# DeltaNet and a multiplicative FFN on one core: another list of steps, with ScalarE's copies of w3 slabs ahead of the first inverse

## The chip, the core and the metric

The kernel runs on one NeuronCore of one Trainium2 chip. The core has five engines that work through their own instruction queues side by side: TensorE (PE in the profile, with its weight loads as PEld), VectorE (DVE), ScalarE (ACT), GpSimd (POOL) and SyncE (SP, which here only issues DMAs). An engine takes its instructions strictly in the order in which the program lists them, and an instruction that needs something from another engine waits at the head of its queue, with everything behind it. The metric is the device time of one execution in microseconds (us).

## What is computed

The reference has two blocks, one behind the other, all in float32. The inputs are q, k, v of shape (4, 8, 768, 48) (batch, heads, tokens, features), beta of (4, 8, 768), and the weights w1, w2 (384 x 1024), w3 (1024 x 1024) and w_out (1024 x 384).

```python
k_n = k / (norm(k) + 1e-6)
for t in range(768):                       # for each batch and head, state is 48 x 48
    y[t]  = q[t] @ state
    state = state + beta[t] * outer(k_n[t], v[t] - k_n[t] @ state)
x = y as (3072 tokens, 384)                # heads side by side
out = ((x @ w1) * (x @ w2)) @ w3 @ w_out   # (3072, 384)
```

## The kernel before

**The recurrence** is done in 12 chunks of 64 tokens. For a chunk, a matrix of products of keys is built for every batch and head, its unit triangular inverse is found, and a few small matmuls then give the chunk's outputs and the next state. Inverses are found for two chunks at a time, on VectorE: a step of elimination is two VectorE instructions (L484 and L489 for the first two pairs of chunks), 31 steps for a pair. The matrix under elimination lies in PSUM, in one of the two double banks that the other small matmuls of the recurrence share.

**The FFN** is linear in h = (x @ w1) * (x @ w2), so w3 @ w_out is multiplied out once: "the fold". w3 comes in 16 pieces of 128 x 512. TensorE transposes each piece (L842), ScalarE brings the result out of PSUM into SBUF (L845), and for each of eight slabs of 128 rows TensorE then accumulates eight matmuls of 384 columns (L856), one for each slab of w_out. The tokens are then worked off 512 at a time (u = 0 to 5): products with w1 and w2, and products with the folded weights. From u = 1 on, and for the folded weights, both use a scheme of Strassen's kind with fewer products and more additions.

All weights arrive as 64-bit pieces of another coding and are turned into float32 on the way: ScalarE does two instructions on a piece (L799, L800), VectorE two (L802, L803), GpSimd one (L807).

**The order of the work** is written out by hand: `ORDER` is a list of 1458 names. Each name stands for a small generator, and each time a name comes up, that generator runs on to its next `yield`; it so adds some instructions to one engine's queue, or to two. At the end `in_text_order()` makes each engine keep exactly this order. In this document P7.3 is the third time that P7 comes up. The names that the change and the prediction speak of are:

- `P0` to `P7`, pieces of w_out; `P8` to `P23`, pieces of w3 (two for each slab of rows: P8 and P9 are slab 0); `P24` to `P35`, pieces of w1 and w2. Each has four steps: .1 the DMA (SP), .2 two ScalarE instructions, .3 two VectorE instructions, .4 one GpSimd instruction. The raw data lie in five buffers that are taken in turn, so the DMA of a piece waits for step .4 of the fifth piece before it.
- `t0` to `t15`: .1 the four transposes of one piece of w3, .2 ScalarE's copy of them into SBUF (L845). t4 and t5 belong to slab 2, t2 and t3 to slab 1.
- `f0` to `f7`: the fold of a slab, .1 its first four and .2 its last four matmuls (two records each in the profile), .3 ScalarE's copy of the result (L863).
- `s m`, `u m`: products of keys of chunk m, with their scaling on VectorE (L395), and the copies that put them in order for the inverse (L446, ScalarE and GpSimd).
- `V j`: the inverse of pair j. For j = 0 and 1: .1 GpSimd writes a unit matrix, .2 VectorE transposes the input (L466), .3 and .4 ScalarE copies the unit matrix into PSUM in two halves (L475), .5 to .35 are the steps of elimination, and .36 is VectorE's transpose of the result (L503).
- `e m`: the inverse is put in place and its corner completed (for chunks 0 to 3 by copies .1 on ScalarE, .2 on GpSimd, .3 on ScalarE, then .4 a VectorE transpose, L559, and from .5 on two products on TensorE with ScalarE copies behind them); `c m`: the chunk's state update, three products (L647) with VectorE work behind each (L678, L687, L707); `y m`: its outputs (L746), brought out by eight ScalarE copies (L767); `d m`: VectorE transposes of keys and queries (L339); `g j`, `N j`: squares and norms of keys; `n m`: GpSimd scales v (L633).
- `b`, `a0`: products of the tokens of u = 0 with w1 and w2 (L876), and for u of 1 to 5 `a`, `h`, `i`, `j` (L995); `S`, `o`, `x`: sums and products with the folded weights (L1105) and results.

PSUM gives the transposes, the fold and the FFN four single banks in turn: each new user waits until the one four before it has been read out.

The fold's lines, with the slab order that the first fold takes:

```python
first = not folded
turn = (0, 3, 2, 5, 1, 4, 6, 7) if first else (0, 3, 2, 1, 5, 4, 6, 7)
for i, kc in enumerate(turn):
    pe.matmul(ps[:, 0:DM], lhsT=w3Ts[jc, kc // 4][:, kc % 4 * P : kc % 4 * P + P],
              rhs=wo[:, kc], start=(i == 0), stop=(i == KF - 1))
    if i == KF // 2 - 1:
        yield
```

So the first slab that is folded needs both of its transposed pieces, and w_out's pieces 0, 3, 2 and 5, for its first half; every later one needs its first piece and w_out's 0, 3, 2 and 1.

Of the kernel before, what the change touches and what calls it, by code (L numbers as in the profile page):

```python
# [43 lines left out]
t4 V0 V0 P5 V0 V0 P4 t10 P7 P4 t3 t3 V0 V0 P1 f1 P6 P6 t4 V0 P7 V0 V0 t10 t1 P14 P7 P4 V0 f0 V0  # L44
P6 P16 P16 V0 V0 P7 t1 s0 P19 P19 P19 P19 V0 f1 P17 k3 p2 v1 V0 V0 P14 P14 P14 V0 f2 P17 f2 f0 V0
f2 P15 v0 P20 f1 t11 f0 P17 P17 f5 V0 V0 P16 t11 P16 t8 P15 V1 V0 t8 f5 t9 V0 V0 t6 P15 V0 n0 n0
f5 V0 V0 V0 V0 t9 P20 P20 V0 t6 P22 P22 P22 f4 P23 P23 V0 f4 f4 P21 P21 P15 t7 t7 V0 s1 V0 V0 V0
V0 g1 d2 d2 P22 f3 f3 P24 P20 g1 g1 p3 g1 P26 p3 P30 e0 e0 e0 t12 t14 e1 e1 g1 f3 e0 e0 d3 d3 N1
s2 s2 s2 P23 P23 t12 e0 f6 e0 p4 s2 P24 e1 e1 t14 s2 e0 P24 s2 P25 c0 P26 f7 u2 P30 P24 c0 e1 e1
P21 P21 d3 d3 y0 y0 P26 P26 P31 t15 t13 s3 s3 s3 s3 s3 s3 t13 c0 n1 n1 P32 t15 u2 u2 u3 c0 P30 f7  # L50
e1 P25 P25 P31 P31 P27 c1 c1 u3 u3 f6 e1 c1 V1 V1 V1 y0 P31 f6 f7 P25 P27 V1 V1 V1 V1 P30 b1 c1
N1 b1 v2 P32 V1 V1 P27 V1 s1 y1 y1 b2 V1 d4 V1 V1 P28 P29 P32 b2 P27 V2 V1 V1 V1 y1 b3 V1 V1 P28
P28 b0 P32 c1 b2 b2 b3 b1 b1 b0 P29 P29 b0 P29 a03 a03 a02 V1 b0 V1 d4 V1 V1 a01 V1 P28 V1 V1 a02
V1 P35 a01 a00 a00 n2 n2 a04 a04 b7 P33 P33 a05 a05 P34 P34 a01 a07 b7 V1 b4 b5 V1 V1 V1 V1 k4
a01 a07 k5 b5 b3 g2 b4 V1 V1 P35 V1 V1 g2 c1 e2 e2 e2 e2 a06 a06 g2 e3 e3 e3 b3 g2 g2 a00 a02 a02
# [12 lines left out]
V3 V3 V3 V3 oB1 xB1 xC1 S1 j20 k9 V3 xD1 V3 V3 V3 V3 S1 oC1 a20 a20 p8 xC1 V3 xC1 h20 V3 xD1 xC1
# [1226 lines left out]
```

## Time and profile before

| | us |
|---|---|
| median of 3 runs (554.44 to 555.08) | 554.49 |
| the profiled execution itself | 556.72 |
| its span, from the first to the last instruction | 555.0 |
| TensorE busy in the span | 523.2 (94%) |
| VectorE busy | 390.5 (70%) |
| GpSimd busy | 257.8 (46%) |
| ScalarE busy | 188.1 (34%) |

The span is what the views of the trace measure; 1.7 us of the profiled execution lie outside it, and it was 2.2 us longer than the median of the runs. A line of a timeline gives an instruction's start and length in us, engine, line, operation, what it writes and reads, its shape, and in square brackets the idle time of the engine before it with what ended it. A line of a table of windows gives, for one stretch, its length, each engine's busy time with the number of instructions, the granted TensorE clock (1.00 is full), the share of the DMA engines and GB/s.

### The profile page before, as it was taken

How to read it: one execution, taken by the hardware profiler on the slowest of the kernel's cores; microseconds unless marked ns; L12 is line 12 of the kernel's file. 1: busy time of each engine (PE TensorE's matmuls, PEld its weight loads, DVE VectorE, ACT ScalarE, POOL GpSimd, SP SyncE). 2: the span in 40 equal slices, each digit the busy share in tenths (PEclk: the TensorE clock that was granted, in tenths of full speed). 3: DMA queues.
4: the chain of work that ended last, by engine and by line, in shares of the span. 5: the costliest groups of instructions: out<-in, count | busy, mean ns of one | idle time of the engine just before them, and what ended most of it. 6: DMA issues, size and time to landing. Idle time of an engine off the chain costs nothing.

```text
span 555.0 us, 19886 instructions
## 1 busy us (share of the span) xinstructions
PE 523.2 (94%) x8540; PEld 449.2 (81%) x8540; DVE 390.5 (70%) x850; ACT 188.1 (34%) x393; POOL 257.8 (46%) x278
## 2 busy tenths in 40 slices
PE   2587999999999999999999999999999999999997
PEld 2473666688778988889987889988899888998897
DVE  3989999899976878659976579858587644124332
ACT  4788288954542112332021530123231121300000
POOL 8585553723658970455443255510382212341141
PEclk9987999999999999999999999999999999999999
DMA  8977976579356445345553564353421220020001
GB/s 248 240 184 195 219 161 127 124 167 146 60 81 116 87 110 81 60 97 92 99 110 61 79 113 65 108 78 47 96 51 44 59 55 4 8 67 1 0 1 57
DMA packets 197688, 52.64 MB, mean 95 GB/s; under 512 B 185345, under 2 KB 191489, under 8 KB 197601
## 3 DMA queue, kind: packets, MB, share of 16 engines
q1 hardware_dynamic: 193408, 50.59, 44.1%
q8 instruction: 67, 1.10, 0.8%
q10 hardware_dynamic: 4192, 0.79, 0.8%
q14 instruction: 21, 0.16, 0.1%
HBM read 41.25 MB, written 8.91 MB: 90 GB/s over the span
## 4 chain that ended last, share of the span: by engine, by line
PE 68%; DVE 11%; DMA 8%; ACT 7%; SPq 2%; issue 2%; POOL 1%; DVEq 0%; POOLq 0%; ACTq 0%
PE ps_f L995 32%; PE ps_f L1105 16%; PE ps_w L647 5%; DMA raw<-in_moe_w_dram 5%; PE ps_w L746 4%; PE ps_w L576 2%; PE ps_w L383 2%; PE ps_f L876 2%; PE ps_w L389 2%; PE ps_f L856 2%; DVE tb L484 1%; DVE tb L495 1%; ACT xT L767 1%; DVE ps_w L489 1%; DVE ps_w L500 1%
## 5 line engine op out<-in xcount | busy, mean ns | idle before, releaser
L1003 DVE TENSOR_TENSOR ab<-ab,ps_f 128x512 f32<-128x512 f32 x80 | 54.6, 683 | 58.1 <-PE ps_f L995 57.5
L1076 POOL TENSOR_TENSOR ab<-ab 128x512 f32<-128x512 f32 (+1 forms) x56 | 61.3, 1118 | 41.0 <-PE ps_f L1105 29.5
L995 PE MATMUL ps_f<-xT,w1s 128*128 128x256 f32 x320 | 78.5, 382 | 0.0
L1042 POOL TENSOR_TENSOR ab<-ab,late 128x512 f32<-128x512 f32 x19 | 24.1, 1270 | 108.2 <-DVE ab L1003 108.2
L995 PEld LDWEIGHTS ps_f<-xT,w1s 128*128 128x128 f32 x320 | 59.9, 190 | 7.9
L1105 PE MATMUL ps_f<-w,ab 128*128 128x192 f32 x376 | 65.6, 329 | 0.0
L1105 PEld LDWEIGHTS ps_f<-w,ab 128*128 128x128 f32 x376 | 61.3, 190 | 1.3 <-issue 0.7
L856 PE MATMUL ps_f<-w2s,w3T 128*128 128x384 f32 x128 | 46.3, 514 | 3.4 <-ACT w3T L845 3.4
L409 POOL TENSOR_TENSOR PT<-PT,smask 128x512 f32<-128x512 f32 x20 | 25.7, 1285 | 51.3 <-ACT PT L407 51.3
L1105 PE MATMUL ps_f<-room,ab 128*128 128x192 f32 x272 | 47.3, 328 | 0.0
L500 DVE TENSOR_TENSOR ps_w<-ps_w,tb 128x31 f32<-128x31 f32 (+15 forms) x124 | 43.3, 349 | 4.3
L767 ACT COPY xT<-ps_w 48x256 f32<-48x256 f32 x96 | 30.4, 365 | 45.2 <-PE ps_w L746 44.7
L495 DVE TENSOR_TENSOR tb<-ps_w,Ub 128x31 f32<-128x31 f32 (+15 forms) x124 | 42.0, 338 | 4.1 <-DMA Ub<-Ud 0.5
L1105 PEld LDWEIGHTS ps_f<-room,ab 128*128 128x128 f32 x272 | 44.3, 190 | 0.6 <-issue 0.3
L1011 ACT COPY ab<-ps_f 128x512 f32<-128x512 f32 x20 | 11.7, 586 | 94.9 <-PE ps_f L995 94.8
L995 PE MATMUL ps_f<-xT,room 128*128 128x256 f32 x160 | 41.2, 385 | 0.0
L856 PEld LDWEIGHTS ps_f<-w2s,w3T 128*128 128x128 f32 x128 | 24.7, 200 | 20.0 <-issue 5.8
L995 PE MATMUL ps_f<-xT,w2s 128*128 128x256 f32 x160 | 40.1, 381 | 0.0
L995 PE MATMUL ps_f<-x_room,w2s 128*128 128x256 f32 x160 | 38.9, 386 | 0.0
L995 PEld LDWEIGHTS ps_f<-x_room,w2s 128*128 128x128 f32 x160 | 29.5, 190 | 5.1 <-DVE late L1003 1.0
L807 POOL TENSOR_TENSOR w<-w,raw 128x512 uint32<-128x512 uint32 x16 | 21.2, 1327 | 26.8 <-DMA raw<-in_moe_w_dram 7.6
L995 PEld LDWEIGHTS ps_f<-xT,room 128*128 128x128 f32 x160 | 29.6, 190 | 4.7 <-DVE osb L1135 0.6
(146 smaller groups left out, 1024.2 us busy)
## 6 DMA issues: line engine op xcount, KB each, us to landing
raw<-in_moe_w_dram SPq DMA_DIRECT2D x16, 512.0 KB, 5.6
vtok<-in_v_dram SPq DMA_DIRECT2D x24, 192.0 KB, 4.2
raw<-in_moe_w_dram SPq DMA_DIRECT2D x24, 192.0 KB, 3.9
out_dram<-osb SPq DMA_DIRECT2D x46, 96.0 KB, 1.7
ktok<-in_k_dram SPq DMA_DIRECT2D x44, 96.0 KB, 3.1
raw<-in_moe_w_out_dram SPq DMA_DIRECT2D x8, 384.0 KB, 3.2
perm<-in_k_dram SPq DMA_DIRECT2D x40, 64.0 KB, 3.0
perm<-in_q_dram SPq DMA_DIRECT2D x32, 64.0 KB, 2.5
```

The lines of the kernel that those rows point to most:

```text
L409: pool.tensor_tensor(out=PT, in0=PT, in1=smask[:].unsqueeze(1).to_broadcast([P, H, C]), op=ALU.mult)
L495: dve.tensor_tensor(out=tv, in0=V[:, 0 : s + 1, s : s + 1].to_broadcast([P, s + 1, n]), in1=U[:, s, s + 1 : BS].unsqueeze(1).to_broadcast( ...
L500: dve.tensor_tensor(out=o, in0=o, in1=tv, op=ALU.subtract)
L647: pe.matmul(out(ps, r, h, z), lhsT=lhs(r, h, z), rhs=rhs(r, h, z), start=True, stop=True,)
L746: i = pe.matmul(region(h, z, r), lhsT=lhs, rhs=rhs, start=part[n] not in part[:n], stop=part[n] not in part[n + 1 :],)
L767: act.copy(out=xT[f, p:NP:2, b : b + NR, cc, :].rearrange("p a r t -> p r a t"), in_=pyv[f, z, b : b + NR],)
L856: pe.matmul(ps[:, 0:DM], lhsT=w3Ts[jc, kc // 4][:, kc % 4 * P : kc % 4 * P + P], rhs=wo[:, kc], start=(i == 0), stop=(i == KF - 1),)
L995: pe.matmul(acc[name][:, n * i : n * i + n], lhsT=ws[b][:, P * i : P * i + P], rhs=xs[x], start=new and k == 0 and i == 0, stop=k == len(t ...
L1003: dve.tensor_tensor(out=o_, in0=x, in1=acc[name], op=ALU.add)
L1042: eng.tensor_tensor(out=Z1, in0=Z1, in1=late, op=ALU.mult)
L1076: pool.tensor_tensor(out=o_, in0=x_, in1=y_, op=op)
L1105: pe.matmul(ps[b][:, b, :], lhsT=block(u, HF * f + i, z)[:, P * b : P * b + P], rhs=ws_[w][:, i], start=first and i == 0 and (b == 0 or n ...
```

## The change

The list is replaced from its 122nd entry on. The same 1458 names come up, each as often as before, so that the same instructions are issued; what differs is their order on each engine, and with it which PSUM bank, buffer or slab each one gets. All other code stays.

At the first difference, ScalarE's copies t3.2, t4.2 and t10.2 come directly behind u1.3. They stood behind V0.3, V0.4, P4.2 and, for the latter two, behind P6.2 and P7.2. ScalarE then goes on with V0.3, P4.2, V0.4, P6.2, P7.2, P14.2. The first fold is that of slab 2 (f2, then f0, f1, f5) where it was slab 1 (f1, then f0, f2, f5). On VectorE, P4.3 comes ahead of the first step of elimination, P14.3 and P16.3 come earlier, and P15.3 later; n0 comes behind P15.4 on GpSimd, where it stood ahead of it. The rest of the list is in another order in most of its lines. Shown are the first 15 lines and the last two that are replaced, and what takes their place (the line ahead of them, the same in both, ends with `P1 u1 u1`; the entry `t4` that the first replaced line begins with is the same too).

```diff
-t4 V0 V0 P5 V0 V0 P4 t10 P7 P4 t3 t3 V0 V0 P1 f1 P6 P6 t4 V0 P7 V0 V0 t10 t1 P14 P7 P4 V0 f0 V0
-P6 P16 P16 V0 V0 P7 t1 s0 P19 P19 P19 P19 V0 f1 P17 k3 p2 v1 V0 V0 P14 P14 P14 V0 f2 P17 f2 f0 V0
-f2 P15 v0 P20 f1 t11 f0 P17 P17 f5 V0 V0 P16 t11 P16 t8 P15 V1 V0 t8 f5 t9 V0 V0 t6 P15 V0 n0 n0
-f5 V0 V0 V0 V0 t9 P20 P20 V0 t6 P22 P22 P22 f4 P23 P23 V0 f4 f4 P21 P21 P15 t7 t7 V0 s1 V0 V0 V0
-V0 g1 d2 d2 P22 f3 f3 P24 P20 g1 g1 p3 g1 P26 p3 P30 e0 e0 e0 t12 t14 e1 e1 g1 f3 e0 e0 d3 d3 N1
-s2 s2 s2 P23 P23 t12 e0 f6 e0 p4 s2 P24 e1 e1 t14 s2 e0 P24 s2 P25 c0 P26 f7 u2 P30 P24 c0 e1 e1
-P21 P21 d3 d3 y0 y0 P26 P26 P31 t15 t13 s3 s3 s3 s3 s3 s3 t13 c0 n1 n1 P32 t15 u2 u2 u3 c0 P30 f7
-e1 P25 P25 P31 P31 P27 c1 c1 u3 u3 f6 e1 c1 V1 V1 V1 y0 P31 f6 f7 P25 P27 V1 V1 V1 V1 P30 b1 c1
-N1 b1 v2 P32 V1 V1 P27 V1 s1 y1 y1 b2 V1 d4 V1 V1 P28 P29 P32 b2 P27 V2 V1 V1 V1 y1 b3 V1 V1 P28
-P28 b0 P32 c1 b2 b2 b3 b1 b1 b0 P29 P29 b0 P29 a03 a03 a02 V1 b0 V1 d4 V1 V1 a01 V1 P28 V1 V1 a02
-V1 P35 a01 a00 a00 n2 n2 a04 a04 b7 P33 P33 a05 a05 P34 P34 a01 a07 b7 V1 b4 b5 V1 V1 V1 V1 k4
-a01 a07 k5 b5 b3 g2 b4 V1 V1 P35 V1 V1 g2 c1 e2 e2 e2 e2 a06 a06 g2 e3 e3 e3 b3 g2 g2 a00 a02 a02
-p4 v3 d4 d4 p5 a00 e2 P34 c2 c2 e2 P34 e2 b6 P35 P35 e2 c2 c2 e3 a03 g2 g2 P33 b6 y2 g2 P33 g2 d5
-d5 p5 c2 c2 y2 a04 e3 s4 N2 e3 s4 a03 s4 b6 b6 s4 s4 s4 s4 T e3 T T d5 n3 d5 a04 e3 b4 b4 b7 s5
-n3 k6 g3 u4 s5 s5 s5 s5 s5 s5 b5 b7 b5 a05 T c3 c3 a06 a05 a06 u5 V2 p6 g3 a07 a07 c3 c3 g3 S0 S0
...
-a53 a53 h53 j53 h51 h53 h53 h53 i53 i53 i53 xC4 o5 x5 o5 S5 S5 o5 o5 x5 S5 S5 S5 S5 o5 x5 x5 o5
-x5 x5 x5 x5 x5 x5 S5 o5 x5 x5 x5 x5
+t4 t10 t3 t3 t4 t10 V0 V0 P5 t1 P4 P4 P1 f2 V0 V0 P4 P7 P14 V0 P6 P6 P6 V0 V0 f0 P7 P14 P14 P16
+s1 P16 V0 P7 V0 V0 P7 P19 f2 P16 P16 f2 P17 P17 k3 P19 t1 f1 f1 V0 V0 f5 V0 f0 P19 f1 p2 v1 V0 f0
+V0 V0 V0 V0 V1 P19 t11 t11 P14 t6 P15 V0 V0 P15 s0 P17 P17 V0 V0 V0 V0 t8 t8 V0 g1 P15 f5 f5 V0
+P15 v0 t9 f4 n0 V0 P20 V0 t6 V0 P20 P20 n1 P22 P22 P23 P21 V0 t7 P22 V0 P22 V0 V0 f3 t9 t7 f4 P20
+t12 P21 V0 V0 g1 g1 e0 n0 e0 e0 g1 d2 g1 d2 f3 f3 e0 e0 t12 s2 e0 e0 N1 t14 f6 P24 P23 p3 e1 P26
+p3 d3 s2 s2 P23 t14 e1 e1 s2 d3 s2 e1 f4 d3 P24 P24 s2 P23 f7 t15 P24 e0 c0 d3 c0 u2 u2 u2 P21
+P21 s1 P26 e1 e1 n1 y0 y0 P26 s3 s3 s3 s3 P30 P30 P30 t15 s3 s3 p4 P25 P31 c0 c0 P25 u3 P26 u3 f7
+P32 u3 P27 t13 P25 c1 c1 e1 t13 f6 V1 V1 V1 V1 V1 V1 V1 e1 c1 y0 f7 V1 V1 c1 N1 P25 b2 y1 V1 P32
+P32 b0 V1 V1 P30 v2 P31 P31 f6 V1 V1 y1 P31 P28 P32 b0 P29 y1 b1 b1 b2 b2 d4 b3 P35 P27 V1 V1 P27
+c1 b1 b3 P28 b0 b2 P27 a02 a02 V1 V1 V1 P28 P28 b1 P29 V1 V1 P33 b0 P29 P35 P29 a03 a03 a01 a01
+V1 d4 V1 P34 k4 a01 V1 V1 k5 b7 b7 a01 a07 a07 g2 V1 V1 a04 V1 V1 V1 V2 a05 a05 a04 a00 a00 b4 V1
+V1 V1 b5 P34 b5 b3 b4 n2 a02 V1 V1 g2 g2 b3 e2 a00 e2 e3 n2 c1 e2 a06 a00 e2 a06 e2 e2 c2 p4 e2
+e2 P34 P34 e3 e3 d4 d4 b6 c2 c2 g2 g2 P35 v3 a02 n3 P33 P33 P33 c2 p5 a03 a03 y2 y2 g2 g2 g2 g2
+P35 b6 b6 T e3 c2 d5 d5 e3 e3 c2 N2 s4 s4 s4 s4 N2 b4 s4 b4 b6 s4 s4 T p5 a04 d5 d5 e3 e3 b7 s5
+s5 T s5 s5 k6 s5 s5 s5 u4 a04 u5 V2 a07 c3 b7 g3 p6 b5 g3 n3 c3 g3 a06 a07 g3 V2 V2 c3 W a05 T c3
...
+h51 a53 a53 h53 a53 a53 a53 j53 h53 h53 h53 h53 i53 i53 i53 o5 o5 x5 o5 S5 o5 S5 S5 o5 x5 x5 S5
+S5 S5 o5 x5 x5 x5 x5 x5 x5 S5 o5 x5 x5 x5 x5 x5
```

## Prediction

> **What bounds the kernel now.** I read the busy shares by slices first. They show a kernel of two parts: TensorE loses time in the first four slices and at the very end, and almost nowhere else; VectorE is at eight or nine tenths in slices 2 to 10 and falls off later.
>
> ```profile
> PE   2587999999999999999999999999999999999997
> DVE  3989999899976878659976579858587644124332
> PEclk9987999999999999999999999999999999999999
> ```
>
> Second, busy time by stretches, cut at the ends of the two first inverses (79.4 and 139.5) and where the FFN takes over (173).
>
> ```profile
> 44.00:79.40 35.40, 32.71 (x106) 19.61 (x107) 33.17 (x85) 21.02 (x40) 18.53 (x18) 0.90 0.86 205
> 79.40:108.00 28.60, 27.10 (x762) 19.35 (x760) 26.13 (x52) 25.79 (x44) 15.99 (x16) 1.00 0.69 143
> 108.00:139.50 31.50, 30.83 (x377) 26.55 (x377) 29.39 (x80) 17.11 (x42) 11.92 (x12) 1.00 0.80 144
> 139.50:173.00 33.50, 31.36 (x969) 26.39 (x968) 25.41 (x55) 16.45 (x34) 23.69 (x27) 1.00 0.46 79
> 173.00:555.00 382.00, 375.94 (x5856) 335.98 (x5848) 243.35 (x526) 77.01 (x180) 154.57 (x162) 1.00 0.33 65
> ```
>
> The third column is TensorE, the fifth VectorE. From 44 to 139.5 both are nearly full, and VectorE's chain (inverse V0, state, inverse V1) cannot be shortened by a faster TensorE. After 173 TensorE alone is the bound: 6.1 us idle in 382, most of it in the tail, so whatever is late at 173 is late at the end.
>
> Third, the timelines around the change. TensorE's fold begins at 40.81, then waits for ScalarE's copy of t3:
>
> ```profile
> 40.81 2.10 PE L856 MATMUL ps_f<-w2s,w3T 128*128 128x384 f32 x6
> 46.03 0.89 PE L856 MATMUL ps_f<-w2s,w3T 128*128 128x384 f32 x2 [3.12 <-ACT w3T L845]
> 48.69 1.65 PE L856 MATMUL ps_f<-w2s,w3T 128*128 128x384 f32 x2 [0.27 <-ACT w3T L845]
> ```
>
> ScalarE is busy all that time, with V0.3 and V0.4 (43.20) ahead of the copy (45.33), and VectorE starts its elimination 0.2 behind them:
>
> ```profile
> 43.20 1.21 ACT L475 COPY ps_w<-Vb 128x512 f32<-128x512 f32 x2
> 44.43 0.55 ACT L799 ACTIVATE w2s<-raw 128x384 f32<-128x384 f32 x1
> 44.88 0.54 ACT L800 ACTIVATE raw<-raw 128x384 uint32<-128x384 uint32 x1
> 45.33 0.56 ACT L845 COPY w3T<-ps_f 128x512 f32<-128x512 f32 x1
> ```
>
> ```profile
> 44.62 0.19 DVE L484 TENSOR_TENSOR tb<-ps_w,Ub 128x31 f32<-128x31 f32 x1
> ```
>
> **The change, part by part.** All instructions stay, so only waits count.
>
> TensorE's side. f2.1 can begin when t4.2 is out: 43.20 plus two copies of 0.52 (three took 1.56 from 37.10 on) is 44.24, against 48.69 for the stretch of fold that ran without a stop. But the work in front of e0.5 is the same six slabs in both lists: 96 records of 0.3225 (16 in 5.16 us, 71.24 to 76.40) are 31.0, six sets of transposes of 0.44 are 2.6, and half a clock at the beginning costs about 3.2; 44.3 + 36.8 = 81.1. e0.5 needs VectorE's e0.4, which before ended at 82.35. So the earlier fold ends in a wait of about 2 us there: gain 0. The new stops inside the fold (t9 waits for f5.3 in the bank, 0.5; t12 for P20.4, about 1) fall into the same wait. If VectorE were not the later one, up to 82.97 - 81.1 = 1.9 would be gained.
>
> VectorE's side, V0's start. ScalarE now does three copies (1.56), V0.3 (0.6), P4.2 (0.99) and V0.4 (0.6) from 43.20 on: 46.95, and the first step comes at 47.15 instead of 44.62. VectorE puts P4.3 (0.96) into the gap, which stood behind that step (0.43). Both were done at 45.97, and will be at 47.58: +1.6. It can't be under 1.0 (P4.3 and the step still both follow ScalarE), and is at most 2.5, if P4.3 isn't done in the gap.
>
> V0's course. P15.3 took 1.02 + 1.20 while GpSimd ran n0 (66.38 to 68.18), where such a pair takes 0.42 + 0.69:
>
> ```profile
> 66.47 1.02 DVE L802 TENSOR_SCALAR w<-w 128x512 uint32<-128x512 uint32 x1
> 67.53 1.20 DVE L803 SCALAR_TENSOR_TENSOR w<-raw,w 128x512 uint32<-128x512 uint32 x1
> ```
>
> ```profile
> 66.38 1.80 POOL L633 TENSOR_TENSOR vtok<-vtok,n 128x384 f32<-128x384 f32 x2
> ```
>
> n0 now stands behind P15.4, so 1.1 is saved (bounds 0, if another GpSimd instruction falls there, and -1.1). The Trainium skill (SBUF — State Buffer, section on the two separate sides) says that the two engines share a port pair which one holds for a whole instruction; by that rule the 1.1 goes, as the row suggests, and each new meeting of a piece's VectorE pair with a GpSimd instruction costs up to that instruction's length. P19.3 needs P19.2, which ScalarE now holds behind f2.3 and so behind f2.2 (44.3 + 24 records + the 3.2 is 55.2): with 0.43, P17.2's 1.25 and 0.68 that is 57.5, and VectorE gets there at 53.77 + 1.6 + 2.3 (P14 and P16 now ahead) = 57.7: nothing, covered by 0.2. V0 ends at 79.40 + 1.6 - 1.1 = 79.9. e0.4 came 2.2 behind V0's end, for its copies. GpSimd now has P22.4, P20.4, g1.7 and n0.2 (1.29, 1.30, 0.83, 0.82) ahead of e0.2, which begins some 0.9 after V0's end and takes 1.2: 2.1 again. So +0.5.
>
> From e0.4 to V1. c0.2 now stands behind d3.3 and d3.4 (0.70 and 0.66), and y0.1 needs c0.2: y0.1 goes from 93.92 to 95.8. From there TensorE has y0.1 (1.1), a wait for y0.2's eight copies, which empty the double bank for s3.4 (2.6), then s3.4, c0.3, f7.2, t13 and c1.1 (1.1, 1.0, 2.8, 0.5, 1.1), with 0.2 of hand-over: c1.1 ends at 106.2, where it was 105.29. So c1.2 and V1.2 are 0.9 late. P31.3 (1.14), which was done ahead of V1.2, is still owed. The work in front of V1's end is the same in both lists, so V1 ends 2.0 late. TensorE agrees: y1.1 waits for c1.4, which now stands behind two more steps (0.63, 0.68): 111.19 + 0.9 + 1.3, +2.2. The bounds of this part: 0.5, if y0.1 were no later, and 3.0, if P26.4 and with it the load P27 and the xT fills behind it in SP's queue are late too (GpSimd now has u2.2 and s1.8, 1.1 and 1.3, ahead of P26.4). In that queue the steps from P7 to v0 keep their order; p4, which waits for d3.2, now has N1, s2.2, s2.3 and P23.3 (3.5, 0.7, 0.7, 1.1) ahead of it on VectorE, so that it goes out at about 90 and not at 87.6, and P25 and P31 behind it at 95 and not at 92.9: nothing, as P25.3 comes at 103.8 and a load took 4.0; if that cover fails it is the same 2.4.
>
> From 139.5 on. TensorE's products of chunk 2 wait for V1, so TensorE's 2.1 idle us there move along. Work in front of e2.5 on TensorE is equal in both lists. I cost the new order behind 173 at nothing: TensorE covers everything there. If that cover fails, a row to bound it by is this 2.1 in 33.5 us; it can give back at most the 2.3 idle us that lie between 173 and the tail.
>
> The sum: +1.6 - 1.1 + 1.5 (from e0.4 to V1's end) = +2.0. Against the profiled execution this is a span of 557.0 and a time of 558.7; against the median of 554.49, which lies 2.2 below that execution's 556.72, **556.5**. No change means within 0.2%, 1.1 us, about what can be measured here.
>
> **Rivals.** *Faster: VectorE loses less between 91 and 106.* There P24, P26 and P30 took 1.33, 1.49 and 1.93 for 1.14, and VectorE waited 0.85 and 0.66 for s3. P30.3 now stands between the two, and GpSimd's u2.2 and u3.2 elsewhere. If all 2.8 go and y0.1 isn't held up, VectorE is at +0.5 - 2.8 = -2.3 at V1: 552.2. It decides if c1.2 begins before 105. Against it: y0.1 needs c0.2, and a wait of VectorE for s3 moves rather than goes. Chance 0.25.
>
> *No change.* The lag is taken up by TensorE's 0.7 and 2.1 idle us between 108 and 173: 554.5. Against it: these are waits for VectorE's own results. Chance 0.15.
>
> *Slower by more, over the clock.* TensorE idles from about 41.3 to 44.3, and the granted clock was 0.50 from 47.2 to 54.0 after a stretch with 0.9 busy us in 3.4.
>
> ```profile
> 43.79:47.20 3.41, 0.89 (x2) 0.30 (x2) 3.13 (x10) 3.36 (x8) 2.16 (x3) 1.00 0.52 175
> 47.20:50.60 3.40, 3.02 (x7) 1.89 (x8) 3.16 (x11) 2.34 (x6) 1.01 (x1) 0.50 0.90 299
> ```
>
> Half a clock costs 0.32 a record. Two such stretches are in my 3.2; four cost 6.4 to 6.8, of which the wait of 2.4 at e0.5 covers part: +1.2 more, 557.7. Chance 0.07. *Slower by more, behind 173*, by a wait such as the 2.1: 558.6. Chance 0.08.
>
> **How the numbers follow.** The forecast, 556.5, has 0.45. Slower by over 0.2% are it and the two last rivals, 0.60; within, 0.15; faster, 0.25. The likeliest's own range is 555.6 to 558. Over all cases I give 551.8, just under the faster rival's 552.2, to 560.0, which adds 1.4 to the last rival: the upper bound of V0's start (0.9) and a third of what SP's queue can add (1.5).
>
> **What would show it.** Right: the first elimination step at about 47; e0.5 on TensorE with a wait for VectorE of 1 to 3 us; V0's end at 79.5 to 80.5; V1.2 at about 107.7; V1's end at 141 to 142; from 173 on the same busy time. Wrong: V0's end before 79.4, V1's end before 139.5, or TensorE's idle time behind 173 changed by over 2 us.

## The result, and the profile after

The changed kernel takes **562.15 us** (median of 4, 559.85 to 562.55) where the kernel before takes 554.79 on the same chip: the ratio is 1.0109, with a 95% interval of 1.0076 to 1.0143. Run once more, beside three of the experiments, it took 561.92 against 556.05 (1.0107, 1.0081 to 1.0134). It is slower, as forecast, but by 7.4 and 5.9 us where the sum gave 2, and it lies above the range.

The busy shares by slices of the changed kernel (PE, DVE, granted clock in tenths):

```profile
PE   2587988889999999999999999999999999999996
DVE  4988899989885986668888479867687645124422
PEclk9859999989999999999999999999999999999999
```

A slice is 14 us. TensorE's slices 6 to 9 (70 to 126 us) have eight tenths where before had nine: the time went there. The same stretches as before, in the same columns:

```profile
44.00:79.40 35.40, 31.71 (x108) 18.41 (x108) 30.90 (x83) 19.29 (x37) 16.54 (x17) 1.00 0.84 200
79.40:108.00 28.60, 24.52 (x753) 18.34 (x754) 27.09 (x50) 24.02 (x41) 18.25 (x18) 1.00 0.65 135
108.00:139.50 31.50, 29.02 (x358) 23.78 (x357) 28.15 (x72) 16.71 (x40) 10.67 (x11) 0.95 0.67 143
139.50:173.00 33.50, 32.27 (x899) 26.79 (x900) 25.93 (x60) 19.81 (x42) 21.48 (x24) 1.00 0.48 70
173.00:555.00 382.00, 380.76 (x5945) 339.24 (x5937) 245.57 (x529) 77.74 (x181) 158.53 (x167) 1.00 0.34 65
```

TensorE's idle time is 4.08 us between 79.4 and 108 (1.50 before) and 2.48 between 108 and 139.5 (0.67 before). From 173 on it is full to the end of the table, because the work that came late is still to be done. In its whole span TensorE is idle for 36.2 us (524.3 busy of 560.5; before 523.2 of 555.0, 31.8 idle): 4.4 more, and as much (4.5) comes from the stretches between 44 and 173.

TensorE's timeline at the two places where it now stands idle, the fold's beginning and the middle of the second inverse:

```profile
44.06 7.36 PE L856 MATMUL ps_f<-w2s,w3T 128*128 128x384 f32 x22 [1.51 <-ACT w3T L845]
53.31 11.23 PE L856 MATMUL ps_f<-w2s,w3T 128*128 128x384 f32 x34 [1.88 <-POOL w2s L807]
...
113.93 2.90 PE L876 MATMUL ps_f<-xT,w1s 128*128 128x256 f32 x6 [2.20 <-ACT raw L800]
116.76 0.85 PE L746 MATMUL ps_w<-KQ,S 48*48 48x64 f32 x32
```

The fold begins at 44.06 and stops for w_out's piece 7 at 51 to 53. The last two lines are b2.1 and y1.1. b2.1 reads xT, which six DMAs of y0.3 fill up; the releaser in the bracket is not an operand of b2.1. Its six records take 2.90 us where six such records took 1.56 before (the first of b1, at 109.07). That part is not the fills but the granted clock (the columns are those of the table of stretches):

```profile
113.80:117.20 3.40, 3.27 (x22) 2.25 (x26) 3.23 (x10) 0.47 (x2) 0.00 (x0) 0.50 0.54 103
```

The queues behind the wait, GpSimd's and SP's:

```profile
103.75 2.41 POOL L807 TENSOR_TENSOR w1s<-w1s,raw 128x512 uint32<-128x512 uint32 x1
```

```profile
96.97 11.75 SPq L791 DMA_DIRECT2D raw<-in_moe_w_dram  x16
108.83 5.04 SPq L778 DMA_DIRECT2D xT<-xT  x6
```

The GpSimd line is P26.4, which began at 97.20 before and now stands behind u2.2 and s1.8. P27's load, the last in SP's group of 16, waits for the buffer that P26.4 frees at 106.16, and the fills wait behind it. They began at 102.74 before. In the second execution of the changed kernel P26.4 took 1.29 instead of 2.41, and the fills began at 107.61.

VectorE's lines where V0 begins, and P15.3:

```profile
45.63 0.36 DVE L802 TENSOR_SCALAR w2s<-w2s 128x384 uint32<-128x384 uint32 x1 [1.37 <-ACT w2s L799]
...
46.56 0.19 DVE L484 TENSOR_TENSOR tb<-ps_w,Ub 128x31 f32<-128x31 f32 x1
...
57.87 0.43 DVE L802 TENSOR_SCALAR w<-w 128x512 uint32<-128x512 uint32 x1 [1.00 <-ACT w L799]
...
70.54 0.42 DVE L802 TENSOR_SCALAR w<-w 128x512 uint32<-128x512 uint32 x1
70.99 0.69 DVE L803 SCALAR_TENSOR_TENSOR w<-raw,w 128x512 uint32<-128x512 uint32 x1
```

In turn: P4.3 waits 1.37 for ScalarE, the first step comes at 46.56, P19.3 waits 1.00, P15.3 has its short length again.

**Where the time is.** Each step of the list was matched with its records by counting along each engine's queue. y1.1, and the start of the second of a02 and a03, are places where TensorE has the same work behind it in every list, so that their lateness is what TensorE has lost. Lateness against before, in us, in two executions of the changed kernel:

| | first | second | forecast |
|---|---|---|---|
| V0's end (79.40 before) | +1.33 | +1.17 | +0.5 |
| V1.2 (106.77) | +1.30 | +2.04 | +0.9 |
| c1.4's end on VectorE (111.13) | +2.76 | +3.50 | +2.2 |
| y1.1 on TensorE (111.19) | +5.57 | +3.49 | +2.2 |
| second of a02 and a03 (124.05) | +5.60 | +4.51 | |
| span (555.0) | +5.5 | +4.4 | +2.0 |

Everything is lost by 130 us. In the first execution y1.1 is 2.8 later than c1.4's lateness explains: about 1.5 is the wait for the fills, and 1.3 is b2.1 at half clock (in run d1 below b2.1 starts at the same 113.93, and at full clock y1.1 follows at 115.40 instead of 116.76). In the second, y1.1 starts right at c1.4's end, and 1.0 is lost between it and a02: 0.47 for a slab of w2, and 0.4 inside y1.1 that no wait in the profile explains. Its lines of TensorE, and c1.4 on VectorE:

```profile
114.68 0.66 PE L746 MATMUL ps_w<-KQ,S 48*48 48x64 f32 x32
...
121.58 0.70 PE L876 MATMUL ps_f<-xT,w2s 128*128 128x256 f32 x2 [0.47 <-POOL w2s L807]
```

```profile
113.68 0.94 DVE L687 TENSOR_TENSOR X<-ps_w,wt 128x768 f32<-128x768 f32 x1
```

### The profile page after: what moved, and what is told of

It reads as the page before. It is cut to its first block, busy times and chain, and to the rows that moved or that the text cites. A ratio compares the mean times of both kernels' runs of the same rounds, so it can differ in the third digit from the quotient of the medians.

```text
span 560.5 us, 19910 instructions
## 1 busy us (share of the span) xinstructions
PE 524.3 (94%) x8540; PEld 449.4 (80%) x8540; DVE 392.8 (70%) x850; ACT 188.6 (34%) x393; POOL 259.0 (46%) x278
## 4 chain that ended last, share of the span: by engine, by line
PE 78%; ACT 7%; DVE 6%; DMA 3%; POOL 2%; issue 1%; SPq 1%; ACTq 0%; DVEq 0%; POOLq 0%
PE ps_f L995 35%; PE ps_f L1105 19%; PE ps_f L876 8%; PE ps_w L647 5%; PE ps_w L746 4%; DMA raw<-in_moe_w_dram 3%; PE ps_w L576 2%; PE ps_w L389 2%; PE ps_w L383 2%; DVE tb L484 1%; ACT raw L800 1%; DVE ps_w L489 1%; ACT KQ L362 1%; SPq L791 1%; ACT w2s L799 1%
## 5 line engine op out<-in xcount | busy, mean ns | idle before, releaser
L856 PE MATMUL ps_f<-w2s,w3T 128*128 128x384 f32 x128 | 43.4, 490 | 3.4 <-POOL w2s L807 1.9
L856 PEld LDWEIGHTS ps_f<-w2s,w3T 128*128 128x128 f32 x128 | 23.5, 190 | 18.7 <-POOL w2s L807 2.5
```

## The experiments

The comparisons of the experiments are with the kernel before on the same chip (medians of 555.9 to 556.4). Their intervals reach 0.8 to 1.7 us to either side, so single effects of under 1 us are read from the traces, and the times only say whether they last. The theories have letters in the order in which they were formed, and each expectation says what its own hold; A is the prediction's reasons with the fills at their upper bound.

| run | ratio, 95% interval | y1.1 | second of a02, a03 | span |
|---|---|---|---|---|
| before | 1 | 111.19 | 124.05 | 555.0 |
| changed | 1.0109 (1.0076, 1.0143) | 116.76 | 129.65 | 560.5 |
| changed, second | 1.0107 (1.0081, 1.0134) | 114.68 | 128.56 | 559.4 |
| a1: fills ahead of P27 | 1.0091 (1.0073, 1.0110) | 115.48 | 129.37 | 560.9 |
| a3: V0 first | 1.0128 (1.0107, 1.0148) | 114.81 | 127.97 | 560.8 |
| a4: a1 and a3 | 1.0103 (1.0083, 1.0122) | 116.87 | 130.74 | 561.1 |
| d1: c1.4 ahead | 1.0107 (1.0088, 1.0127) | 115.40 | 128.73 | 559.7 |
| e1: a1 and d1 | 1.0111 (1.0091, 1.0132) | 114.63 | 129.54 | 560.5 |
| g1: c0.2 ahead | 1.0126 (1.0100, 1.0151) | 116.17 | 130.04 | 561.1 |
| h1: e1.2 ahead | 1.0107 (1.0084, 1.0130) | 115.22 | 129.10 | 560.6 |
| f1: before's list to e0.5 | 1.0078 (1.0053, 1.0103) | 114.60 | 127.40 | 558.9 |
| s1: before's list to c1.3 | 1.0067 (1.0042, 1.0091) | 113.76 | 126.46 | 557.5 |
| s1c: s1 and c1.4 ahead | 1.0053 (1.0034, 1.0071) | 112.40 | 125.10 | 557.0 |
| s2: changed list to c1.3 | 1.0139 (1.0108, 1.0170) | 118.11 | 132.29 | 562.0 |
| b1: before, copies first | 1.0018 (1.0003, 1.0034) | 111.62 | 124.33 | 554.0 |
| d3: before, c1.4 behind | 1.0009 (0.9990, 1.0029) | 112.70 | 125.41 | 555.7 |
| e5: before, fills ahead | 1.0007 (0.9992, 1.0022) | 109.95 | 123.06 | 553.7 |
| n0 and c1.4 in before | 1.0006 (0.9986, 1.0026) | 112.83 | 127.01 | 556.7 |
| e4: that, and fills ahead | 1.0008 (0.9991, 1.0024) | 110.40 | 124.25 | 554.2 |
| h2: before, e1.2 behind | 0.9998 (0.9983, 1.0013) | 111.15 | 124.00 | 553.6 |

### The start of V0

b1 does the change's first part alone, in the list of before:

```diff
-t4 V0 V0 P5 V0 V0 P4 t10 P7 P4 t3 t3 V0 V0 P1 f1 P6 P6 t4 V0 P7 V0 V0 t10
+t4 t10 t3 t3 t4 t10 V0 V0 P5 V0 V0 P4 P7 P4 V0 V0 P1 f1 P6 P6 V0 P7 V0 V0
```

> The kernel before with one part of the change alone: ScalarE's and VectorE's copies t10.1, t3.1, t3.2, t4.2 and t10.2 stand ahead of V0.2, so the slabs of w3T are out before V0 goes on; the fold's and all other orders are those of before. Theory A: the first elimination step moves from 44.62 to 46 to 47, V0 ends 1 to 1.6 late, and the time is 0.8 to 1.6 over before: 555.3 to 556.4. Rival (the earlier copies let TensorE begin the fold sooner, and this reaches e0.5): faster than before by 0.5 or more. A second rival: V0's delay is taken up by the slack that VectorE has from 80 to 100, and the time is within 0.5 of before.

a3 undoes a part of it in the changed list (V0.2 to V0.4 stand ahead of the copies again, P4.2 stays behind them):

```diff
-t4 t10 t3 t3 t4 t10 V0 V0 P5 t1 P4 P4 P1 f2 V0 V0
+t4 t10 t3 V0 V0 V0 t3 t4 t10 P5 t1 P4 V0 P4 P1 f2
```

> The changed kernel with V0.2 to V0.4 on ScalarE and VectorE put ahead of the second w3T copy (t3.2) again, and V0.5 ahead of P4.3, as before has them; the fold's order stays. Theory A (VectorE is late from V0's start): the first elimination step starts near 44.7 instead of 46.56, V0 ends near 79.3 instead of 80.73, and 1.3 to 2.0 us are carried to c1.3; behind it the fills still start at P26.4's end, which moves by as much, so the kernel gains 1 to 2: 560 to 561. The fold begins 1 to 2 us later than 44.06. Theory B (what counts is behind V1): the gain of the start is taken up by the wait at b2.1, under 0.5 in all. Theory C (clock): the fold's later start leaves TensorE idle longer at 43 to 46 and the half clock stays up to 4 us longer, the gain is nothing or a loss of up to 1.

b1 is 1.0 us slower than before (0.2 to 1.9), within theory A's 0.8 to 1.6. Its trace is of the fastest of its 12 runs (555.75) and shows less than the theory had: VectorE waits where it should, but the first step comes at 45.43 and not at 46 to 47, the step and P4.3 are both done at 46.86, 0.9 later than before, and V0 ends at 79.18, no later than before, since P15.3 met no n0 in this execution (more on that below).

```profile
45.43 0.19 DVE L484 TENSOR_TENSOR tb<-ps_w,Ub 128x31 f32<-128x31 f32 x1 [1.51 <-ACT ps_w L475]
```

But undoing it gains nothing. In a3 V0 begins at 44.75, 1.8 earlier, and VectorE waits for P4.2 right behind the first step instead:

```profile
44.75 0.19 DVE L484 TENSOR_TENSOR tb<-ps_w,Ub 128x31 f32<-128x31 f32 x1
46.60 0.36 DVE L802 TENSOR_SCALAR w2s<-w2s 128x384 uint32<-128x384 uint32 x1 [1.42 <-ACT w2s L799]
```

V0 ends at 80.61 (80.73 and 80.57 in the changed kernel). The three copies are in front of P4.2 in either order, and VectorE's list has P4.3 in front of the second step: what ScalarE owes is paid at one of two places. At P19.3 the two lists are level (57.72 and 57.87): the changed kernel waits 1.00 there, a3 does not. So V0.3's and V0.4's place alone does not count while P4.2 stays behind the copies; a list that moves P4.2 as well was not run.

### The two waits at y1.1

a1 lets y0.3's fills go ahead of P27's load on SP; a4 has a1's and a3's moves:

```diff
-f7 P32 u3 P27 t13 P25 c1 c1 e1 t13 f6 V1 V1 V1 V1 V1 V1 V1 e1 c1 y0 f7
+f7 P32 u3 t13 P25 c1 c1 e1 t13 f6 V1 V1 V1 V1 V1 V1 V1 e1 c1 y0 P27 f7
```

> The changed kernel with one step moved: P27's load on SP's queue stands behind the third group of xT fills (y0.3) instead of ahead of it, so the fills no longer wait for GpSimd's P26.4. Theory A (the fills): of the 7.4 us that the changed kernel lost, some 3.0 came up between c1.3 (2.58 late) and the second part of y1 (5.57 late), because b2's six matmuls waited for these fills. Then y0.3 starts near 104 to 105 instead of 108.83, the wait of 2.20 us ahead of b2.1 and the stretch of its six records (2.90 against 1.56 us) go, V1 ends near 140.5 instead of 143.38, and the kernel is 2 to 3.5 us faster than the changed one: 558.5 to 560, still about 4 over before. Theory B (the loss is in the lists behind V1, the fills only happen to be late): VectorE or GpSimd is late at b2.1 anyway, the wait gets another name, and the time stays within 0.7 of the changed kernel's 561.8. Theory C (the clock: the changed kernel ran 17.1 us at half clock ahead of the fold and 3.4 us behind b2.1's wait): only the 3.4 us stretch goes, worth about 0.5 to 1.5.

> The changed kernel with both moves of the two kernels before: V0's first steps ahead of the w3T copies, and y0.3 ahead of P27's load on SP's queue. Theory A: the two causes stand one behind the other in time and so add up: 3.5 to 5.5 faster than the changed kernel, 556.5 to 558.5, with V1's end at 139 to 140. What is left against before (some 2) would be from P26's, u2's and s1's new order on GpSimd and from c0.2 behind d3.3. Theory B: no more than 1 faster in all. Theory C (clock): 0 to 1.5 faster.

d1 puts c1.4 ahead of V1.9 and V1.10 on VectorE; e1 has a1's and d1's moves:

```diff
-e1 c1 y0 f7 V1 V1 c1 N1 P25 b2 y1
+e1 c1 y0 f7 c1 V1 V1 N1 P25 b2 y1
```

> The changed kernel with one instruction moved: c1.4 (VectorE's product into X, which y1.1 on TensorE reads) stands ahead of V1.9 and V1.10 again, as before has it. Theory E, new: TensorE's loss behind c1.3 is c1.4's place. In the changed order V1.9 and V1.10 (1.34 us in the first splice) stand ahead of it, and y1.1 started at 114.68 right at c1.4's end 114.63 in the second run of the changed kernel. Then c1.4 ends 1.3 earlier, y1.1 starts up to 1.3 earlier where the fills are in (the fills hold b2.1 in some executions, and there it gains less), and the time is 0.6 to 1.5 below the changed kernel's 1.0107 times before: ratio 1.008 to 1.0096. Rival (V1's end on VectorE sets what follows, the sum of VectorE's work ahead of it is the same): within 0.4 of the changed kernel, ratio 1.010 to 1.0115.

> The changed kernel with both moves: y0.3's fills ahead of P27 on SP's queue, and c1.4 ahead of V1.9 and V1.10 on VectorE. Theory G (two waits side by side): with the fills early and c1.4 late y1.1 began at 115.48, right at c1.4's end 115.43; with c1.4 early (end 113.41) and the fills late b2.1 ahead of y1.1 began at 113.93 only, and y1.1 at 115.40. Each alone hid the other; with both gone y1.1 starts right behind c1.3 and b2.1, 1.2 to 2.5 earlier than in the changed kernel, and 0.8 to 2.0 of it are left at the end: ratio to before 1.007 to 1.0095. Rival H (V1's end on VectorE, the sum of its work, sets what follows): V1.36 ends where it did (142.5 to 143.4) and the time is within 0.4 of the changed kernel: ratio 1.010 to 1.0115.

None of the four is clearly faster than the changed kernel; a1 comes nearest, and its interval still holds 1.0107. The lines of TensorE tell why. In a1 the fills start at 104.39, b2.1 takes its 1.56, and y1.1 then waits for c1.4 (which is itself 1.5 later than in the first execution, since VectorE's c1.2 waited 2.12 for TensorE's c1.1 here, behind a stretch at half clock):

```profile
113.19 1.56 PE L876 MATMUL ps_f<-xT,w1s 128*128 128x256 f32 x6
115.48 0.67 PE L746 MATMUL ps_w<-KQ,S 48*48 48x64 f32 x32 [0.73 <-DVE X L687]
```

In d1 c1.4 ends at 113.41, and b2.1 waits for the fills (they start at 107.53):

```profile
113.93 1.53 PE L876 MATMUL ps_f<-xT,w1s 128*128 128x256 f32 x6 [1.55 <-ACT raw L800]
115.40 0.67 PE L746 MATMUL ps_w<-KQ,S 48*48 48x64 f32 x32
```

So the two are side by side, which is e1's theory G. In e1 both are gone, and the next wait is b2.3's, for the two slabs that P31.4 and P32.4 finish on GpSimd at 121.26 and 122.51:

```profile
121.32 0.70 PE L876 MATMUL ps_f<-xT,w2s 128*128 128x256 f32 x2 [1.13 <-POOL w2s L807]
122.56 0.70 PE L876 MATMUL ps_f<-xT,w2s 128*128 128x256 f32 x2 [0.55 <-POOL w2s L807]
```

The list of before has P31.2 and P31.3 ahead of c1.2 (P31.3 at 104.84); the changed one has them behind y1.1 (116.97 in its first execution). That is a third wait behind the first two. And e1, like a1 and a4, ran TensorE at half clock just ahead of all this; columns as in the table of stretches:

```profile
94.40:101.20 6.80, 4.24 (x261) 3.84 (x254) 6.42 (x9) 5.36 (x14) 5.53 (x5) 1.00 0.70 151
101.20:104.60 3.40, 3.40 (x96) 3.00 (x89) 3.27 (x6) 3.35 (x6) 3.20 (x5) 0.54 0.97 219
```

V1.2 came 29.40 us behind V0's end there, against 27.34 and 28.24 in the two executions of the changed kernel.

### c1.4 and the fills in the list of before

d3 is d1's mirror: in before, c1.4 goes behind V1.10, and nothing else changes on any engine:

```diff
-V1 V1 V1 P30 b1 c1 N1 b1 v2 P32 V1 V1 P27
+V1 V1 V1 P30 b1 N1 b1 v2 P32 V1 V1 c1 P27
```

> The kernel before with one instruction moved: c1.4 stands behind V1.10 instead of ahead of V1.9, as in the changed list; TensorE's, ScalarE's, GpSimd's and SP's orders are those of before, to the instruction. Theory E: y1.1's wait for X grows from 0.55 to about 1.9 us, and the 1.35 us stay to the end: 1.0 to 1.5 over before (ratio 1.0018 to 1.0027). Rival: V1's end on VectorE stays where it is (139.47), TensorE makes up the wait by what it does until then, and the time is within 0.4 of before.

The lines of y1.1 in before, and then in d3:

```profile
111.19 0.67 PE L746 MATMUL ps_w<-KQ,S 48*48 48x64 f32 x32 [0.55 <-DVE X L687]
```

```profile
112.70 0.66 PE L746 MATMUL ps_w<-KQ,S 48*48 48x64 f32 x32 [1.27 <-DVE X L687]
```

y1.1 comes 1.51 later, the second of a02 and a03 1.36 later, and the span is 0.7 longer; the time, +0.5 us, can't be told from none. So c1.4's place costs 1.4 us at y1.1, and half of it was made up later in this execution.

e5 takes the fills ahead of P27 in before (SP's order alone changes):

```diff
-P27 c1 c1 u3 u3 f6 e1 c1 V1 V1 V1 y0
+c1 c1 u3 u3 f6 e1 c1 V1 V1 V1 y0 P27
```

> The kernel before with P27's load behind y0.3's fills on SP's queue; all other engines' orders are those of before. Theory G: the fills start near 101.5 instead of 102.74 and land ahead of b1.1 at 109.07 in every execution; in the profiled execution of before they did so anyway, so the fast executions stay and the late ones (up to 558.9 where the median is 556) go: the median falls by 0 to 0.8, the largest by more. P27's pieces come in up to 3 us later, beside ScalarE's P27.2 at 108.87, which may then wait: a loss of up to 0.5. Rival: the spread has another origin, and median and spread stay as they are.

They start at 98.70 instead of 102.74 and the time stays (1.0007): in the order of before they are not what TensorE waits for.

### Which part of the list

Three spliced lists take the first entries from one kernel and the rest, in its order, from the other:

```diff
+s1: the first 340 entries of before (to c1.3), then the changed order
+s2: the first 346 entries of the change (to c1.3 and y0.3), then the order of before
+f1: the first 265 entries of before (to e0.5), then the changed order
+s1c: s1 with c1.4 ahead of V1.9 and V1.10
```

> The changed kernel once more, on the chip of the three kernels beside it, so that they can be set against it directly. Expected as first measured: 1.0109 times before's median, some 5 to 7 us over it, about 562 to 564 where before reads 556.4.

> Spliced list: before's order for the first 340 entries (to c1.3 and V1's first steps, with P26.4 and P27.1 where before has them), the changed order for all steps that are then left. Theory A as it stands after the first runs: with the fills ahead of P27 the time from c1.3 to V1.36 was 29.92 against 31.55 us in the changed kernel and 30.22 before, so the fills were worth 1.6, not 3.0; c1.3's own lateness of 2.6 is carried to V1's end undiminished. Both lie ahead of the splice, so this kernel has c1.3 near 108.0 and V1's end near 139.5 and is 0 to 1 over before. Theory B: the changed order behind c1.3 costs by itself (TensorE had waited 3.9 us between y1.1 and a02 in before, 5.1 in all three kernels with the changed order even where the fills were early): 1.2 to 2.5 over before.

> The opposite splice: the changed order for the first 346 entries (through c1.3 and y0.3, P27.1 ahead of it), before's order for all steps that are then left. Theory A: c1.3 is near 110.6 and the fills near 108.8 as in the changed kernel, V1 ends 3.5 to 4.5 late, and the time is within 1 of the changed kernel's, 4.5 to 6 over before. Theory B: the loss behind c1.3 is saved, the time is 1.5 to 2.5 below the changed kernel's. The two splices' differences from before should add up to the whole difference within 1.5, if the two parts do not act on each other.

> A third splice: before's order for the first 265 entries (V0, the fold and P15 with them, to e0.5), the changed order for all that is left. Theory A: V0's 1.3 us are saved, e0.4 ends near 82.35; what then lies between e0.5 and c1.3 (GpSimd's u2 and s1 ahead of P26.4, c0.2 behind d3.3) costs as in the changed kernel, c1.3 is 1.0 to 1.6 late, y0.3 still waits for P27: the time is 1 to 2 below the changed kernel's. Rival: the start's lateness is not the cause of c1.3's (VectorE would be late by u2, d3 and n0 alone): no more than 0.5 below.

> The first splice (before's order to c1.3, the changed order behind it, 1.0067 times before) with c1.4 ahead of V1.9. Of its profile's 2.41 us that TensorE had lost more than in before at the end, 1.34 were V1.9 and V1.10 ahead of c1.4, and 1.0 was P31.3's pair, stretched to 2.11 (1.15 in before) beside GpSimd. Theory E: y1.1 starts near 112.4 instead of 113.76, the time is 1.0 to 1.5 below the splice's, ratio 1.004 to 1.005. Rival: no more than 0.4 below, ratio 1.006 to 1.0067.

s1 is 3.7 us over before (2.3 to 5.1): theory A's "0 to 1" fails. The order behind c1.3 costs by itself, with c1.3 in time (108.14; 108.00 before) and the fills nearly so (103.31; 102.74). In the trace it is the wait for c1.4:

```profile
113.76 0.67 PE L746 MATMUL ps_w<-KQ,S 48*48 48x64 f32 x32 [2.36 <-DVE X L687]
```

Of the 2.57 that y1.1 is late, 1.36 go when c1.4 is put ahead (s1c: 112.40). Of the other 1.21, 0.97 is P31.3, whose second instruction took 1.66 in s1 and 0.69 in before. The time falls from 1.0067 to 1.0053, by less than the intervals can tell. s1c is still 2.9 over before; its trace has 1.05 of that at the second of a02 and a03, and the rest is not explained.

s2 is 7.7 over before, more than the whole change. So the two parts do not add up (3.7 + 7.7 against 5.9): the order of before behind c1.3 fits late predecessors worse than the changed one does. In the trace of s2 that is b1.1, which waits 2.52 for P25.4: GpSimd has it behind P31.4 there, and P31.3 comes at 113.01. f1, with V0, the fold and P15 as before, is 4.3 over: that part of the change is worth some 1.6 of 5.9, with each end uncertain by more than 1. But its trace does not give V0 the part that theory A does. V0 ends 0.22 earlier than before, and V1.2 is still 0.87 late and c1.3 2.15, where A had 1.0 to 1.6. VectorE's c1.2 ahead of them waits for TensorE's c1.1; here it is in the first execution of the changed kernel, and then in f1:

```profile
107.20 0.95 DVE L678 TENSOR_TENSOR vtok<-vtok,ps_w 128x768 f32<-128x768 f32 x1 [0.48 <-PE ps_w L647]
```

```profile
106.77 0.95 DVE L678 TENSOR_TENSOR vtok<-vtok,ps_w 128x768 f32<-128x768 f32 x1 [0.50 <-PE ps_w L647]
```

In all eleven executions that have the changed order from e0.5 to c1.3 (some with the single moves told here), c1.2 waits there, for 0.39 to 2.27; in the nine with the order of before it waits 0.07 at most. So in this stretch the changed list is late on TensorE, whether V0 is late or not.

### Two smaller suspects between e0.4 and c1.4

g1 puts c0.2 ahead of d3.3 and d3.4 on VectorE, which the prediction had made the cause of y0.1's lateness:

```diff
-f4 d3 P24 P24 s2 P23 f7 t15 P24 e0 c0 d3 c0
+f4 P24 P24 s2 P23 f7 t15 P24 e0 c0 c0 d3 d3
```

> The changed kernel with c0.2 (VectorE) ahead of d3.3 and d3.4, as before has it. The prediction's step: d3.3 and d3.4 hold c0.2 and so y0.1, which TensorE waits for; then c0.2 ends some 1.3 earlier (95.3 to 95.5 instead of 96.6 to 96.8), y0.1 starts 1.0 to 1.3 earlier, and 0.6 to 1.3 are left at the end: ratio 1.0085 to 1.0097. Theory F (between e0.4 and c1.4 VectorE's sum of work counts, and this order leaves the sum as it is): y0.1 is earlier, c1.4 and y1.1 are not, and the time is within 0.4 of the changed kernel: ratio 1.010 to 1.0115.

It is no faster (1.0126). c0.2 does not come earlier; it waits for its product:

```profile
96.09 0.96 DVE L687 TENSOR_TENSOR X<-ps_w,wt 128x768 f32<-128x768 f32 x1 [1.17 <-PE ps_w L647]
```

TensorE's c0.1, which makes it, starts at 94.62 in the first execution of the changed kernel and at 89.51 in before, since the changed list has f7.1 and t15.1 ahead of it. The transposes d3.3 and d3.4 only filled VectorE's wait. From there the lateness stays on TensorE: y0.1 is 2.9 late and c1.1, which c1.2 waits for, 1.8.

h1 and h2 look at one small instruction. In both executions of the changed kernel, the second instruction of N1.1 takes 1.14 instead of 0.19 and ends with GpSimd's e1.2; VectorE's and GpSimd's lines, second execution:

```profile
83.69 1.14 DVE L301 SCALAR_TENSOR_TENSOR nt<-ss,seed 128x32 f32<-128x32 f32 x1
```

```profile
83.68 1.10 POOL L549 COPY TT<-Ub 32x512 f32<-32x512 f32 x1
```

```diff
-f3 e0 e0 t12 s2 e0 e0 N1 t14 f6 P24 P23 p3 e1 P26 p3 d3 s2 s2 P23 t14 e1 e1
+f3 e0 e1 e1 e0 t12 s2 e0 e0 N1 t14 f6 P24 P23 p3 P26 p3 d3 s2 s2 P23 t14 e1
```

(h1, in the changed list) and

```diff
-t12 t14 e1 e1 g1 f3 e0 e0 d3
+t12 t14 e1 g1 f3 e0 e0 e1 d3
```

(h2, in the list of before).

> The changed kernel with e1.1 and e1.2 (the copies into TT on ScalarE and GpSimd) ahead of e0.5, as before has them. Theory K (the meeting of N1.1 with e1.2 makes VectorE 0.95 late, and VectorE sets all that follows to c1.4): N1.1 takes 3.5, c0.2 ends 0.95 earlier, P26.3, P26.4 and the fills as well, and 0.6 to 1.0 are left at the end: ratio to before 1.0085 to 1.0097. e1.1 on ScalarE (some 1.1) now stands ahead of a w3T copy and of e0.6's copies, which may take back up to 0.5. Rival: the lateness is taken up by the next meeting or wait (P21.3, P26.3, c1.2 for c1.1), and the time is within 0.4 of the changed kernel: 1.010 to 1.0115.

> The kernel before with one instruction moved: e1.2 (GpSimd, 1.1 us) behind e0.5's; all orders but GpSimd's are those of before, to the instruction. Theory K: N1.1's first L301 meets it and takes 1.1 instead of 0.19, N1.1 takes 4.4 instead of 3.46, c0.2 ends 0.9 later, and 0.5 to 0.9 of it last to the end: ratio 1.0009 to 1.0016. Rival: VectorE's idle time of 0.85 and 0.66 ahead of s3.2 and s3.5 takes it up, c1.4 ends where it did, and the time is within 0.3 of before.

In h1 N1.1 takes 4.10 instead of 4.49, but s2.4 behind it on TensorE starts where it did (90.05; 90.13), since TensorE has lost 1.38 at e0.7 to ScalarE, and the time stays at 1.0107. In h2 e1.2 was over at 82.51, ahead of N1.1, so the meeting did not come about and h2 tells nothing on it.

### A better list

The last two kernels take into before what the traces showed as a gain and a cheap repair: n0 behind P15.4, c1.4 ahead of V1.8, and for e4 the fills ahead of P27.

```diff
-P15 V0 n0 n0 f5
+P15 V0 f5
...
-P21 P21 P15 t7 t7
+P21 P21 P15 n0 n0 t7 t7
...
-V1 V1 V1 V1 P30 b1 c1
+V1 V1 V1 c1 V1 P30 b1
```

> The kernel before with what the runs showed of the change's gain and of its loss: n0's two GpSimd instructions behind P15.4 (P15.3's pair took 2.26 beside them in before, 1.14 in the changed kernel), and c1.4 ahead of V1.8, one V1 step earlier than before has it (TensorE's wait of 0.55 for X at y1.1). Theory E: V0's end and e0.4 come 1.1 earlier, of which 0.3 to 1.1 reach c1.3, and y1.1's wait of 0.55 goes: 0.6 to 1.6 below before, ratio 0.997 to 0.999. Rival: what VectorE gains at P15 it loses to GpSimd at the next meeting (n0 then beside V0's last steps or P20), and V1's end is where it was: within 0.4 of before.

> The kernel before with n0 behind P15.4, c1.4 ahead of V1.8, and P27's load behind y0.3's fills. Without the last of these three the profile had V0's end 1.0 earlier and c1.3 0.5 earlier, and lost it at the fills (y0.3 104.73 instead of 102.74, b2.1 waiting 1.8). Theory G: with the fills early c1.3's 0.5 and y1.1's wait of 0.55 are saved to the end: 0.5 to 1.2 below before, ratio 0.998 to 0.999. Rival H: the gain is taken up by VectorE's later work, within 0.4 of before.

Neither beats before (1.0006, 1.0008), nor does any other kernel here. In the first, V0 ended 1.0 earlier, and the fills, at 104.73 in that execution, took it back; in e4 V0's end and y1.1 are earlier (78.35, 110.40), and the time is the same.

## Why the prediction was wrong

**V0's start, +1.6: right as a mechanism, and the first step came within 0.6 of the forecast 47.15.** P4.3 and the first step were both done 1.0 and 1.5 late, inside the bounds of 1.0 and 2.5. b1 has the delay alone, 0.9 in its trace. What a3 adds is that it makes no difference to V0's end whether V0.3 and V0.4 stand ahead of the copies or behind them.

**P15, -1.1: right against the profiled execution only.** The pair took 1.14. But the meeting that it removes is not there in every execution of before. n0 also waits for v's load, and in five of the eight executions here whose list has n0 where before has it, it came too late to meet P15.3; b1's:

```profile
67.36 0.42 DVE L802 TENSOR_SCALAR w<-w 128x512 uint32<-128x512 uint32 x1
67.81 0.69 DVE L803 SCALAR_TENSOR_TENSOR w<-raw,w 128x512 uint32<-128x512 uint32 x1
```

Against a median the term is near nothing. It is one reason why the measured difference, 7.4 and 5.9 us, is larger than that of the spans, 5.5 and 4.4; the profiled execution of before was 2.2 over its median.

**P19.3, "nothing, covered by 0.2": wrong by 1.00 and 0.4** in the two executions. VectorE was there 0.8 and 0.4 before the forecast 57.7, and what P19.3 needs of P19.2 came 0.4 and 0.2 after the forecast 57.5. With that V0's end was 1.33 and 1.17 late, not 0.5.

**The fold's earlier beginning, 0: right** in that it brought nothing, but not by its sum. The wait at e0.5 was 0.28 and 0.26, not 1 to 3, since the six slabs were done at 83.46 and 83.30, not at 81.1. In the first execution the 3.2 for half a clock did not come (the fold ran at full clock), and stops of 4.45 stood in its place; 1.88 of them, for w_out's piece 7, the prediction did not list. In the second, one stretch of 3.4 us was at half clock, and piece 7 cost 0.18.

**From e0.4 to V1's end, +1.5: the step that failed.** V1.2 (+0.9 forecast, +1.30 and +2.04 measured) does come late through TensorE's c1.1, as the prediction had it: c1.2 waits 0.48 and 1.12 for it. But c0.2 behind d3.3 and d3.4, the reason given, is not it (g1); c0.2 waits for c0.1, which stands behind f7.1 and t15.1 on TensorE. Nor does it take V0's lateness (f1). c1.4 behind two more steps, +1.3, is right: 1.46 in the changed kernel, 1.36 in s1 against s1c. But the sum stopped at y1.1's forecast +2.2, and took what followed to be equal. What was missing is a third loss behind c1.4, of 1.0 to 2.8. In the first execution 1.5 of it is the fills behind P26.4 and P27, the mechanism that the prediction named for its upper bound of 3.0 and kept out of its sum, and 1.3 is the half clock that followed that wait. In the second 0.47 is the slab of P32, which TensorE's b2.3 waits for, and the rest has no wait to show for it; the 1.14 of P31 that the prediction had as owed on VectorE it did not have as something that b2.3 waits for. With +2.8 the step would have been 4.3 and the span 560; the other number at fault is V0's end.

**SP's late p4, P25, P31, "nothing": right** as far as these loads go.

**Behind 173, nothing: right.** From the second of a02 and a03 on, the changed kernel's lateness moved by 0.1 (5.60 to 5.5, 4.51 to 4.4).

**The rivals.** *Faster*: in the first execution VectorE did lose its two waits for s3 of 0.85 and 0.66, but not the stretched pieces (P26.3 took 2.12, P25.3 2.11), and c1.2 began at 107.2, not before 105. *No change* fell with the result. *Slower over the clock*, with 0.07, put it at the fold, where it did not come; it came at 101 to 104.6 and at 113.8 to 117.2, in some executions.

**What stays open.** The closed account is that of two executions' traces. That no single repair, and neither of the two pairs tried, gives the time back is shown; that all of them together would is not, since no list with all was run. Why the changed order behind c1.3 alone costs 3.7, of which the trace of s1 shows 2.5, is not settled; why the two halves do more harm apart than together is read from one trace of s2 alone.

## What to carry to other kernels

When a list is reordered in a stretch where three engines are nearly full, write down for the next few places all operands and their arrival, not only the one that came last: with one wait removed the next took its place, three times over. An upper bound that names a concrete mechanism (a queue, a buffer, who frees it) belongs into the sum if each of its links is late by the same trace. And a gain read from one execution's meeting of two engines is worth what it is in the other executions, so look at what the later of the two waits for: a DMA's landing makes the meeting a matter of chance.

## What the runs showed of the hardware

**Half clock behind a gap.** In five of the eleven executions that have the changed order from e0.5 to c1.3 (a1, a4, e1, g1, h1), the granted clock in 101.2 to 104.6 was 0.50 to 0.69; in none of the nine with the order of before there. TensorE was busy for 4.24 to 4.89 of the 6.8 us ahead of it in ten of these eleven, and for 5.43 to 5.83 in the nine. The gap does not decide alone: the second execution of the changed kernel had 4.26 and kept its clock. In e1 f7.2's eight records then took 3.53 (2.85 before), and c1.1 stands behind them: c1.2 waited 1.58 to 2.27 for it in the five and 0.39 to 1.12 in the other six. V1.2 came 29.1 to 29.6 us behind V0's end in the five, instead of 27.3 to 28.5. So the changed order costs about one to two further microseconds in some executions. The Trainium skill (TensorE: Matmul & The Clock Gate, Part 1) says that the gate judges a free-running window of about 3.4 us; the trace agrees as to the length (0.50 from 113.8 to 117.2 in the changed kernel), and that the same gap has different consequences would follow from where the window falls, which no run here shows.

**A small instruction can wait out a large one.** N1.1's 0.19 became 1.14, up to the end of GpSimd's copy, though it moves only 32 elements a partition. The Trainium skill (SBUF — State Buffer, SBUF: two separate sides) has it that the port pair is held for the whole instruction, and the row agrees; in h1 no instruction of N1.1 was stretched beyond 0.42.

**The mean granted clock says little of the time.** It lay between 0.981 and 0.997 in the 17 runs of before beside a1, and the run at 0.981 took 555.65 us, one at 0.997 took 557.69. The mean does not say where half a clock falls: of the 20.5 us at 0.50 in the first execution of the changed kernel, 17.1 end at 42.1, ahead of the fold, and only 3.4 lie where the time was lost.
